# Two tiles of x loaded through the ScalarE queue, and one tile's transposes placed ahead of the first gate matmuls

## The chip, the cores and the metric

The kernel runs on one core of a Trainium2 chip. The metric is device time in microseconds (us) of one execution; the kernel before took 179.11 us as the median of 6 runs (178.76 to 179.28). Names of engines in the profile: PE is TensorE (matmuls, and PEld its weight loads), DVE is VectorE, ACT is ScalarE, POOL is GpSimd, SP is SyncE. DMA transfers are issued either by SP's queue (SPq in the profile) or by ACT's (ACTq).

## The reference

The input is normalised, and two branches work on the normalised rows: a state-space recurrence and a gated feed-forward. The sum of both and the input is the output.

```python
xn = _layernorm(x, axis=-1)                       # x: 1 x 2048 x 512, bf16
# A: 512 complex states; Lam, B, C, dt are parameters
Lam_bar = jnp.exp(dt * Lam)
B_bar = ((Lam_bar - 1.0) / Lam)[:, None] * Bmat
Bu = jnp.einsum("bld,pd->blp", xn + 0j, B_bar)
for t in range(L):                                # L = 2048
    h = Lam_bar[None, :] * h + Bu[:, t, :]
y = 2.0 * jnp.einsum("blp,dp->bld", hseq, Cmat).real + xn * Dskip
# B: w_gate, w_up: 512 x 1376, w_down: 1376 x 512
ffn = (_gelu(xn @ w_gate) * (xn @ w_up)) @ w_down
out = x + y + ffn
```

## The kernel before, in words

The 2048 rows are 16 tiles of 128 rows, taken in four blocks of four tiles. For each block the kernel normalises (LN), transposes the rows through DMA (TR, so that the 512 columns lie on the partitions), multiplies with the gate and up weights (GU), multiplies with B (BU), runs the recurrence as scans on DVE (CHAIN) and multiplies hidden values and states with w_down and C into one accumulation (DN). The blocks are interleaved so that PE always has something to do.

Block 0 can't wait for DMA transposes, so its head goes another way, and the change is in this head only. Each of its tiles j is centred on DVE (`sub`, line 932; for tile 1 line 940, whose mean comes from ACT, line 937), transposed by PE against an identity (`cent_T(j)`, line 673: four 128x128 transposes) and copied from PSUM by ACT (line 680; for tile 0 in two halves, in two banks). Then `GT_mm(j, r, bank, us, ks)` (line 698) multiplies the transposed tile with column range r of the gate (us has 0) or up (us has 1) weights over the quarters ks of the 512 inputs. `GT_evac` (lines 707 and 710) applies gelu on ACT and the product on DVE.

Before the first tile is there PE runs 7 matmuls of 512 columns on zeros (`fwarm`, line 913), and between the first real steps it runs `fill(n)`, n matmuls of 128 columns on zeros into a spare bank (line 920). Their results are not used.

In what follows x0 to x3 are the loads of tiles 0 to 3 (`ld_x0`, line 498, 128 KB each), gate half 0 and gate half 1 the two loads of the first 384 gate columns (`ld_wg0`, line 502, 192 KB each), WU0 the load of the first 384 up columns (line 494). The three small parameter rows (line 518) go through the ACT queue and are transposed by a DMA (`tr_par`, line 522), which SP issues after the weights and before the four transposes of block 0 (TR(0), line 722).

The kernel has its own planner (`Sched`). PE's and SP's instructions run in the order in which the program makes them; those of DVE, ACT and POOL are put in order by a list scheduler that uses a guessed duration for each operation (`dur`) and the dependencies, in six rounds, of which the shortest plan is kept. `order_behind(op, prev)` puts op behind prev on the same engine with no semaphore wait. Waits are made for all other dependencies. `after=[...]` adds a dependency by hand. The gelu on one column at line 480 has no use for its value: it makes ACT load its gelu table early. Its guessed duration is 1480 ns.

The order of PE's head is written by hand:

```python
fill(2)
cent_T(0, tb, "AA")
fill(3)
... # gate, tile 0, quarters 0 and 1, r = 0 and 1
cent_T(1, [wb])
... # gate, tile 0, quarters 2 and 3
fill(6)
...
for r in range(2):
    GT_mm(1, r, ub[1, r], [0])
```

On DVE the head is a chain in fixed order (`ch`): statistics of tile 0, its centring, tile 1's centring, statistics of tile 1, root, statistics and centring of tile 2, reciprocal, two normalisations, tile 3.

Of the kernel before, what the change touches and what calls it, by code (L numbers as in the profile page):

```python
# [10 lines left out]
ACTF = mybir.ActivationFunctionType  # L11
# [356 lines left out]
D_TINY = 160.0  # L368
def d_act(n, ptr=0): return 190.0 + 0.833 * n + 90.0 * ptr
# [3 lines left out]
def build(nc, ins, out):  # L373
    with ExitStack() as es:
        E = es.enter_context
        S = Sched(nc, es)
# [6 lines left out]
        def ring(parent, name, n):  # L383
            return [A.sub(parent, "%s%d" % (name, i), i) for i in range(n)]
# [13 lines left out]
        X = ring(X_all, "X", NT)  # L398
# [18 lines left out]
        HALF = A.alloc("HALF", [4], F32)  # L417
# [11 lines left out]
        PROWq = [Buf("PROW%d" % q, "prow", q, q + 1) for q in range(3)]  # L429
# [39 lines left out]
        x2 = ins["A_x"][0]  # L469

        V = lambda fn, dur, r, w, tag="", after=(): S.op("vector", fn, dur, r, w, tag, after)
        ACT = lambda fn, dur, r, w, tag="", after=(): S.op("scalar", fn, dur, r, w, tag, after)
# [3 lines left out]
        V(lambda e: e.memset(WRM.ap, 0.0), 150, [], [WRM], "wrm")  # L476
        GATE = {"before_gelu": [], "nh": 0}
        SCR = A.alloc("SCR", [1], F32)
        V(lambda e: e.memset(HALF.ap, 0.5), D_TINY, [], [HALF], "half")  # L479
        GATE["table"] = ACT(lambda e: e.activation(SCR.ap, HALF.ap[:, 0:1], ACTF.Gelu_apprx_tanh), 1480, [HALF], [SCR], "gelu0")  # L480
        POOL(lambda e: e.iota(IOT.ap, [[1, 128]], base=0, channel_multiplier=-1), 300, [], [IOT], "iota")
        GATE["ident"] = V(lambda e: e.tensor_scalar(IDN.ap, IOT.ap, 0.0, None, ALU.is_equal), d_dve_ts4x(128), [IOT], [IDN], "ident")
        POOL(lambda e: e.memset(PROW16.ap, 0.0), 100, [], [PROW, *PROWq], "prow0")
# [8 lines left out]
        def ld_w(W, Wc, src, ci, queue="sync", after=()):  # L492
            f0, f1 = FCH[ci]
            return S.dma(lambda e: e.dma_start(W.ap[:, :, f0:f1], src[:, f0:f1].rearrange("(k p) f -> p k f", p=128)),
                         512 * (f1 - f0) * 2, writes=[Wc[ci]], tag="ld_w", queue=queue, after=after)

        def ld_x0(j):
            S.dma(lambda e, j=j: e.dma_start(X[j].ap, x2[128 * j:128 * (j + 1), :]), 128 * 1024, writes=[X[j]], tag="ld_x0")
        WG0h = [Buf("WG0h%d" % n, "sbx", n / 2, (n + 1) / 2) for n in range(2)]

        def ld_wg0(n, queue, after=()):
            return S.dma(lambda e: e.dma_start(WG.ap[:, 2 * n:2 * n + 2, 0:384],
                                        ins["B_w_gate"][256 * n:256 * (n + 1), 0:384].rearrange("(k p) f -> p k f", p=128)),
                  192 * 1024, writes=[WG0h[n]], tag="ld_w", queue=queue, after=after)
        ld_x0(0)
        ld_x0(1)
        ld_wg0(0, "sync")
        ld_wg0(1, "scalar", [GATE["iotj"]])
        ld_x0(2)
        ld_w(WU, WUc, ins["B_w_up"], 0)  # L510
        ld_x0(3)
        for ci in (1, 2):
# [3 lines left out]
        def load_par():  # L516
            for q, nm in enumerate(("A_log_dt", "A_Lambda_re", "A_Lambda_im")):
                S.dma(lambda e, q=q, nm=nm: e.dma_start(PROW.ap[4 * q:4 * q + 4, :], ins[nm].rearrange("(s p) -> s p", p=128)),
                      1024, writes=[PROWq[q]], tag="ld_" + nm, queue="scalar", after=[GATE["iotj"]])

        def tr_par():
            S.dma(lambda e: e.dma_start_transpose(PAR.ap.rearrange("p q t -> p (q t)").unsqueeze(1), PROW16.ap), 4096,
# [34 lines left out]
        def next_bank():  # L557
            b_ = rstate["n"] % 8
            rstate["n"] += 1
            return b_  # L560
# [102 lines left out]
        def cent_T(j, banks, engs="A"):  # L663
            per = KD // len(engs)
            for n, eng in enumerate(engs):
                bank = banks[n]
                pt = PS[bank].bitcast(BF16)

                def f(e, n=n, pt=pt):
                    ins_ = None  # L670
                    for q in range(per):
                        k = per * n + q
                        ins_ = e.transpose(pt[:, 128 * q:128 * (q + 1)], XN[j].ap[:, 128 * k:128 * (k + 1)], IDN.ap)  # L673
                    return ins_
                PE(f, 56.0 * per, [XN[j], IDN], [BANK[bank]], "T0")
                dst = XC_all.ap[:, per * n:per * (n + 1), 128 * j:128 * (j + 1)]
                src = pt[:, 0:128 * per].rearrange("p (q t) -> p q t", q=per)
                w = [XCs[j][n]] if len(engs) == 2 else XCs[j]
                if eng == "A":
                    GATE["evTA"] = ACT(lambda e, src=src, dst=dst: e.activation(dst, src, ACTF.Copy), d_act(128 * per), [BANK[bank]], w, "evT")  # L680
                else:
                    V(lambda e, src=src, dst=dst: e.tensor_copy(dst, src), 110 + 0.6 * 128 * per, [BANK[bank]], w, "evT")
# [3 lines left out]
        def GT_mm(j, r, bank, us, ks=range(KD)):  # L686
            f0, f1 = FR[r]
            w = f1 - f0
            ci = max(0, r - 1)
            Wc = [(WGc, WUc)[u][ci] for u in us]  # L690
            if ci == 0 and us == [0] and len(ks) == 2:
                Wc = [WG0h[ks[0] // 2]]
            dst = PS[bank][:, w * us[0]:w * (us[-1] + 1)].rearrange("p (w f) -> p w f", w=len(us))

            def f(e):
                ins_ = None
                for k in ks:
                    ins_ = e.matmul(dst, XCd(j, k), WGU[:, us[0]:us[-1] + 1, k, f0:f1], start=(k == 0), stop=(k == KD - 1))  # L698
                return ins_
            PE(f, d_pe([w * len(us)] * len(ks)), Wc + XCs[j][ks[0] // 2:ks[-1] // 2 + 1], [BANK[bank]], "GT")  # L700
# [207 lines left out]
        wb = next_bank()  # L908
# [7 lines left out]
        def fill(n):  # L916
            def f(e):
                ins_ = None
                for _ in range(n):
                    ins_ = e.matmul(PS[fb][:, 0:128], WRM.ap, WRM.ap, start=True, stop=True)  # L920
                return ins_
            PE(f, 56.0 * n, [WRM], [BANK[fb]], "fill")
# [8 lines left out]
        def sub(j):  # L931
            return V(lambda e: e.tensor_scalar(XN[j].ap, X[j].ap, MVt[0][j].ap[:, 0:1], None, ALU.subtract),
                     d_dve_ts4x(512), [X[j], MVt[0][j]], [XN[j]], "sub")
        load_par()
        load_W()
        tr_par()
# [9 lines left out]

        fill(2)
        cent_T(0, tb, "AA")
        fill(3)
        ub = {(j, r): next_bank() for j in range(2) for r in range(2)}  # L950
        for r in range(2):
            GT_mm(0, r, ub[0, r], [0], (0, 1))
        cent_T(1, [wb])
        for r in range(2):
            GT_mm(0, r, ub[0, r], [0], (2, 3))
        fill(6)
        for j in range(2):
            ch(norms(0, [j], mn0, rq0, 0))
        ch(*stats(0, 3)); ch(sub(3))
# [64 lines left out]
def bass_parallel_sum__ssm_conv_s5__geglu_ffn__prompt_kernel(  # L1024
    nc: bass.Bass,
    A_x: bass.AP,
    A_Lambda_re: bass.AP,
    A_Lambda_im: bass.AP,
    A_B_re: bass.AP,
    A_B_im: bass.AP,  # L1030
    A_C_re: bass.AP,
    A_C_im: bass.AP,
    A_log_dt: bass.AP,
    A_Dskip: bass.AP,
    B_x: bass.AP,
    B_w_gate: bass.AP,
    B_w_up: bass.AP,
    B_w_down: bass.AP,
    out: bass.AP,
):  # L1040
    ins = {
        "A_x": A_x, "A_Lambda_re": A_Lambda_re, "A_Lambda_im": A_Lambda_im,
        "A_B_re": A_B_re, "A_B_im": A_B_im, "A_C_re": A_C_re, "A_C_im": A_C_im,
        "A_log_dt": A_log_dt, "A_Dskip": A_Dskip,
        "B_w_gate": B_w_gate, "B_w_up": B_w_up, "B_w_down": B_w_down,
    }
    build(nc, ins, out)
# [28 lines left out]
```

## Time and profile before

| what | value |
|---|---|
| median of 6 runs | 179.11 us |
| the profiled execution: time | 178.76 us |
| the profiled execution: span in the trace | 177.0 us |
| PE busy | 173.2 us, 98% of the span |
| DVE busy | 160.7 us, 91% |
| ACT busy | 89.3 us, 50% |
| POOL busy | 10.0 us, 6% |
| DMA moved | 14.36 MB, mean 81 GB/s |

The span goes from the first instruction to the last one of the trace; the execution's own time is 1.76 us more. Times inside the trace count from the span's start. The busy time of PE says that it has work queued nearly always, not what the work is: the warm matmuls and fills of the head count in it too. The page's 40 slices show PE at 9 tenths in all slices but the first (7) and the last (3), and DVE at 9 in most slices after the second. The DMA engines are at 9 tenths in slices 2 to 5, which is 4.4 to 22 us, and mostly at 4 or below after slice 14.

### The profile page before, as it was taken

To read this page: it belongs to the slowest core of one execution; us is meant where nothing else is said; L and a number is where in the kernel's file an instruction comes from. 1 tells how busy PE (TensorE), PEld (TensorE's weight loads), DVE (VectorE), ACT (ScalarE), POOL (GpSimd) and SP (SyncE) were. 2 spreads that over 40 slices of the span, in tenths; PEclk is the share of its full clock that TensorE was granted. 3 is DMA by queue.
4 is the path that set the end of the run, shared out by engine and by line. 5 is a ranking of instruction groups with operands and counts; after the bars stand their busy time and mean duration, and the time that the engine had idled before them with its cause. 6 is when DMAs were issued, how large, how long until landed. Compare 5 with 4: busy or idle time off the path is not lost.

```text
span 177.0 us, 2522 instructions
## 1 busy us (share of the span) xinstructions
PE 173.2 (98%) x893; PEld 84.6 (48%) x893; DVE 160.7 (91%) x283; ACT 89.3 (50%) x169; POOL 10.0 (6%) x25
## 2 busy tenths in 40 slices
PE   7999999999999999999999999999999999999993
PEld 3854464444644444444644444444554444444453
DVE  4989999996999999789999999899999999999911
ACT  4475578989866897003676593000757680000000
POOL 3212030220000000300000000000000000000000
PEclk9999999999999999999999999999999999999999
DMA  5999989286799400011034000100001000000321
GB/s 150 322 323 91 256 203 159 33 162 133 155 196 337 50 0 0 0 61 59 4 66 82 2 0 0 33 30 30 30 0 33 0 0 0 0 0 25 103 86 30
DMA packets 33396, 14.36 MB, mean 81 GB/s; under 512 B 23688, under 2 KB 33384, under 8 KB 33384
## 3 DMA queue, kind: packets, MB, share of 16 engines
q1 hardware_dynamic: 33088, 14.00, 34.7%
q10 hardware_dynamic: 296, 0.20, 0.4%
q8 instruction: 7, 0.11, 0.3%
q14 instruction: 5, 0.04, 0.1%
HBM read 6.46 MB, written 2.10 MB: 48 GB/s over the span
## 4 chain that ended last, share of the span: by engine, by line
PE 98%; DVE 0%; issue 0%
PE PS L863 37%; PE PS L823 32%; PE PS L734 16%; PE PS L698 7%; PE PS L797 3%; PE PS L913 2%; PE PS L673 1%; PE PS L920 0%; DVE arena L881 0%; DVE arena L476 0%; DVE arena L479 0%
## 5 line engine op out<-in xcount | busy, mean ns | idle before, releaser
L863 PE MATMUL PS<-arena 128*128 128x512 bf16 (+3 forms) x323 | 66.2, 366 | 0.0
L823 PE MATMUL PS<-arena 128*128 128x512 bf16 x264 | 58.1, 379 | 0.0
L863 PEld LDWEIGHTS PS<-arena 128*128 128x128 bf16 (+1 forms) x323 | 30.9, 98 | 35.2
L823 PEld LDWEIGHTS PS<-arena 128*128 128x128 bf16 x264 | 25.8, 98 | 30.4
L767 DVE TENSOR_TENSOR_SCAN arena<-arena 128x512 bf16<-128x512 f32 x32 | 38.7, 1250 | 0.0
L838 ACT ACTIVATE arena<-PS 128x512 bf16<-128x512 f32 x33 | 19.8, 600 | 37.4 <-PE PS L823 32.9
L734 PE MATMUL PS<-arena 128*128 128x512 bf16 x128 | 28.1, 379 | 0.0
L841 ACT ACTIVATE arena<-PS 128x512 bf16<-128x512 f32 x33 | 19.9, 602 | 5.0 <-PE PS L823 5.0
L734 PEld LDWEIGHTS PS<-arena 128*128 128x128 bf16 x128 | 12.5, 98 | 14.9
L855 ACT ACTIVATE PS<-arena 128x512 f32<-128x512 bf16 (+2 forms) x17 | 9.3, 580 | 17.5 <-DVE arena L881 17.1
L738 ACT ACTIVATE arena<-PS 128x512 bf16<-128x512 f32 x32 | 17.4, 599 | 1.2 <-PE PS L734 1.0
L881 DVE TENSOR_TENSOR arena<-PS,arena 128x512 bf16<-128x512 f32 (+2 forms) x17 | 10.9, 654 | 7.6 <-PE PS L863 7.4
L843 DVE TENSOR_TENSOR arena<-arena 128x512 bf16<-128x512 bf16 x33 | 13.0, 411 | 1.9 <-ACT arena L841 1.9
L698 PE MATMUL PS<-arena 128*128 128x192 bf16 (+2 forms) x80 | 13.0, 315 | 0.1
L624 DVE BATCH_NORM_STATS2 arena<-arena 128x6 f32<-128x512 bf16 x16 | 10.2, 681 | 1.2 <-DMA arena<-in_A_x_dram 1.2
L698 PEld LDWEIGHTS PS<-arena 128*128 128x128 bf16 x80 | 7.2, 98 | 4.9 <-issue 0.3
L756 DVE TENSOR_TENSOR arena<-arena 128x4096 bf16<-128x4096 bf16 (+1 forms) x5 | 9.2, 1861 | 0.1
L754 DVE TENSOR_TENSOR arena<-arena 128x4096 bf16<-128x4096 bf16 (+1 forms) x5 | 9.2, 1854 | 0.0
L780 DVE TENSOR_TENSOR arena<-arena 128x4096 bf16<-128x4096 bf16 x4 | 9.1, 2283 | 0.0
L779 DVE TENSOR_TENSOR arena<-arena 128x4096 bf16<-128x4096 bf16 x4 | 9.1, 2282 | 0.0
L707 ACT ACTIVATE arena<-PS,arena 128x192 bf16<-128x192 f32 (+1 forms) x16 | 6.7, 449 | 3.0 <-PE PS L698 3.0
L710 DVE SCALAR_TENSOR_TENSOR arena<-PS,arena 128x192 bf16<-128x192 f32 (+1 forms) x16 | 6.9, 447 | 1.1 <-ACT arena L707 0.6
(84 smaller groups left out, 110.6 us busy)
## 6 DMA issues: line engine op xcount, KB each, us to landing
out_dram<-arena SPq DMA_DIRECT2D x15, 128.0 KB, 1.7
arena<-in_A_x_dram SPq DMA_DIRECT2D x3, 512.0 KB, 5.0
arena<-in_B_w_down_dram SPq DMA_DIRECT2D x1, 1280.0 KB, 7.9
arena<-in_A_x_dram SPq DMA_DIRECT2D x4, 128.0 KB, 2.7
arena<-in_B_w_gate_dram SPq DMA_DIRECT2D x2, 256.0 KB, 4.8
arena<-in_B_w_up_dram SPq DMA_DIRECT2D x2, 256.0 KB, 5.1
arena<-in_B_w_gate_dram SPq DMA_DIRECT2D x1, 480.0 KB, 5.6
arena<-in_B_w_up_dram SPq DMA_DIRECT2D x1, 480.0 KB, 5.9
```

The lines of the kernel that those rows point to most:

```text
L624: return (V(lambda e: e.bn_stats(ST[tt].ap, X[tt].ap), d_dve_1x(512), [X[tt]], [ST[tt]], "bnst"), V(lambda e: e.bn_aggr(MVt[b][j].ap, ST[t ...
L698: ins_ = e.matmul(dst, XCd(j, k), WGU[:, us[0]:us[-1] + 1, k, f0:f1], start=(k == 0), stop=(k == KD - 1))
L734: ins_ = e.matmul(PS[bank][:, :], BBT[c][dk].ap[:, 128 * s:128 * (s + 1)], XNT[b].ap[:, dk, :], start=(dk == 0), stop=(dk == KD - 1))
L738: ACT(lambda e, bank=bank, k3=k3, s=s, c=c: e.activation(SSc[k3][s][c].ap, PS[bank][:, :], ACTF.Copy), d_act(512), [BANK[bank]], [SSc[k3][ ...
L767: V(lambda e, g=g, rb=rb, init=init: e.tensor_tensor_scan(g.ap, rb, g.ap, init, ALU.mult, ALU.add), d_dve_scan(512), [g, PA[RRr]] + ([CARc ...
L823: ins_ = e.matmul(PS[bank][0:m, c0:c1], W.ap[:, dk, 128 * ft:128 * ft + m], XNT[b].ap[:, dk, c0:c1], start=(dk == 0), stop=(dk == KD - 1))
L838: GATE["last_gelu"] = ACT(lambda e, bg=bg, kk=kk, m=m: e.activation(GG[kk].ap[0:m, :], PS[bg][0:m, :], ACTF.Gelu_apprx_tanh), d_act(512), ...
L841: ACT(lambda e, bu=bu, kk=kk, m=m: e.activation(UPB[kk].ap[0:m, :], PS[bu][0:m, :], ACTF.Copy), d_act(512), [BANK[bu]], [UPB[kk]], "evU")
L843: V(lambda e, kk=kk, m=m, ft=ft, k2=k2: e.tensor_tensor(HTt[k2][ft].ap[0:m, :], GG[kk].ap[0:m, :], UPB[kk].ap[0:m, :], ALU.mult), d_dve_tt ...
L855: ACT(lambda e: e.activation(PS[bank][:, c0:c1], X[tt].ap[:, c0:c1], ACTF.Copy), d_act(c1 - c0), [X[tt]], [BANK[bank]], "seed")
L863: ins_ = e.matmul(PS[bank][:, c0:c1], l_[:, 128 * j:128 * (j + 1)], r_[:, c0:c1], start=False, stop=last and n == len(ops) - 1, skip_group ...
L881: V(lambda e: e.tensor_tensor(OUTB[ko].ap[:, c0:c1], PS[bank][:, c0:c1], XD[tt].ap[:, c0:c1], ALU.add), d_dve_1x(c1 - c0), [BANK[bank], XD ...
```

## The change

Three things are changed, all in the head.

1. x1 and x2 are issued from the ACT queue, ordered behind the table gelu, instead of from SP's. Gate half 1 goes the other way, from the ACT queue (where it waited for `iotj`, an iota on POOL) to SP's. SP's order is then x0, gate half 0, gate half 1, WU0, x3 and so on.
2. The three parameter rows wait for `half` (a memset on DVE) instead of for `iotj`, beside the memset of their target, which stays. The table gelu's guessed duration goes from 1480 to 100 ns; the instruction is the same.
3. On PE tile 1's transposes go ahead of tile 0's gate matmuls, in the place of `fill(3)`, and `fill(6)` becomes `fill(4)`.

```diff
-        V(lambda e: e.memset(HALF.ap, 0.5), D_TINY, [], [HALF], "half")
-        GATE["table"] = ACT(lambda e: e.activation(SCR.ap, HALF.ap[:, 0:1], ACTF.Gelu_apprx_tanh), 1480, [HALF], [SCR], "gelu0")
+        half = V(lambda e: e.memset(HALF.ap, 0.5), D_TINY, [], [HALF], "half")
+        GATE["table"] = ACT(lambda e: e.activation(SCR.ap, HALF.ap[:, 0:1], ACTF.Gelu_apprx_tanh), 100, [HALF], [SCR], "gelu0")
...
-        def ld_x0(j):
-            S.dma(lambda e, j=j: e.dma_start(X[j].ap, x2[128 * j:128 * (j + 1), :]), 128 * 1024, writes=[X[j]], tag="ld_x0")
+        def ld_x0(j, queue="sync", after=()):
+            return S.dma(lambda e, j=j: e.dma_start(X[j].ap, x2[128 * j:128 * (j + 1), :]), 128 * 1024, writes=[X[j]], tag="ld_x0", queue=queue, after=after)
...
         ld_x0(0)
-        ld_x0(1)
+        S.order_behind(ld_x0(1, "scalar"), GATE["table"])
         ld_wg0(0, "sync")
-        ld_wg0(1, "scalar", [GATE["iotj"]])
-        ld_x0(2)
+        ld_wg0(1, "sync")
+        S.order_behind(ld_x0(2, "scalar"), GATE["table"])
         ld_w(WU, WUc, ins["B_w_up"], 0)
         ld_x0(3)
...
-                      1024, writes=[PROWq[q]], tag="ld_" + nm, queue="scalar", after=[GATE["iotj"]])
+                      1024, writes=[PROWq[q]], tag="ld_" + nm, queue="scalar", after=[half])
...
         fill(2)
         cent_T(0, tb, "AA")
-        fill(3)
+        cent_T(1, [wb])
         ub = {(j, r): next_bank() for j in range(2) for r in range(2)}
         for r in range(2):
             GT_mm(0, r, ub[0, r], [0], (0, 1))
-        cent_T(1, [wb])
         for r in range(2):
             GT_mm(0, r, ub[0, r], [0], (2, 3))
-        fill(6)
+        fill(4)
```

## The prediction

> **What bounds the kernel now.** I read the chain of work that ended last first, then PE's waits, then the head instruction by instruction on PE, DVE and ACT, then the DMA. By the chain PE holds 98% of the span. Its pieces in the head (start, duration, what):
>
> ```profile
> 4.37 0.46 PE PS L673 x4
> 4.83 0.24 PE PS L920 x3
> 5.07 0.11 issue
> 5.18 0.49 PE PS L698 x4
> 5.67 0.22 PE PS L673 x4
> 5.89 0.33 PE PS L698 x4
> 6.22 0.34 PE PS L920 x6
> 6.56 0.02 issue
> 6.58 1.17 PE PS L698 x12
> ```
>
> L673 are transposes, L698 real matmuls, L920 fills. From 6.58 to 174.3 the chain has no step off PE. The list of PE's waits has one entry in the whole span, the start:
>
> ```profile
> PE PS L913 <- DVE arena L479: 1.0, 1, 1.0
> ```
>
> So time can be won only ahead of 6.58, where fills and holes are not work, and can be lost anywhere. What releases PE there is on ACT and DVE (start, duration, engine, line):
>
> ```profile
> 3.39 0.63 ACT L937 ACTIVATE arena<-arena 128x512 bf16<-128x512 bf16 x1 [1.16 <-DMA arena<-in_A_x_dram]
> 3.93 0.18 ACT L937 ACTIVATION_READ_ACCUMULATOR arena<-arena 128x1 f32 x1
> 4.22 0.35 DVE L940 TENSOR_SCALAR arena<-arena 128x512 bf16<-128x512 bf16 x1
> 4.65 0.38 ACT L680 ACTIVATE arena<-PS 128x256 bf16<-128x256 bf16 x1 [0.54 <-PE PS L673]
> 4.93 0.38 ACT L680 ACTIVATE arena<-PS 128x256 bf16<-128x256 bf16 x1
> 5.93 0.60 ACT L680 ACTIVATE arena<-PS 128x512 bf16<-128x512 bf16 x1 [0.62 <-PE PS L673]
> ```
>
> Tile 1: x1's landing, its mean on ACT (to 4.11), centring on DVE (to 4.57). Centred tile 1 then lies idle until 5.50, when its transposes start. Their copy ends at 6.53, and tile 1's matmuls start at 6.58: fill(6) (to 6.56) only covers that wait. The first gate matmul (5.18) waits for tile 0's first copy, done at 5.03.
>
> **The change, part by part.** The sum is made in the profiled execution (178.76 us, span 177.0, 0.35 under the median of the runs); I carry its difference to the median, 179.11.
>
> *PE's order.* Tile 0's transposes stay where they are, to 4.83. Tile 1's follow at once, 0.22 by their own row, to 5.05. They sit in the 0.35 that fill(3) and the hole take, so gate matmuls still start at 5.18: 0.13 behind the transposes. First quarters 0.49 (to 5.67), second 0.33 (to 6.00), with the 0.22 between them gone. fill(4) is 4 x 0.34/6 = 0.23, to 6.23. Tile 1's copy: transposes end at 5.05, ACT is free for the next copy 0.28 after 4.93 (the spacing of its first two), so 5.21 to 5.81, below 6.23. Tile 1's matmuls start at 6.23 instead of 6.58: 0.22 + 2 x 0.057 + 0.02 = **0.35 won**.
>
> *x1's landing decides whether that holds.* The trace's semaphore updates put landings at 2.84 (x0, issued 0.74), 3.37 (x1, issued 1.19), 4.72 and 4.96 (gate halves 0 and 1), 5.29 (x2). Centred tile 1 is there 4.57 - 3.37 = 1.20 after x1, and PE needs 0.06 more (4.16 to 4.22 for tile 0). Transposes that start at landing + 1.26 end at landing + 1.48; the gate matmuls move only when that is past 5.18, so a landing up to 3.70 costs nothing. Past it PE stands still us for us, and at 3.70 + 0.35 = 4.05 the gain is gone. Behind the mean's wait for x1 on ACT stand tile 0's copies: they start at 4.65, and the mean's 0.72 ends by then for a landing up to 3.93.
>
> *The ACT queue.* It waits for `half` (0.88 to 0.94), so x1 is issued at some 1.0. The table load doesn't hold it:
>
> ```profile
> 0.74 1.28 ACT L480 ACT_TABLE_LOAD   x1 [0.74 <-PEq L1061]
> 1.61 0.50 ACTq L502 DMA_DIRECT2D arena<-in_B_w_gate_dram  x1
> 2.03 0.20 ACT L480 ACTIVATE arena<-arena 128x1 f32<-128x1 f32 x1
> ```
>
> The queue issued at 1.61, in the load, and the gelu still ran right behind the load: it had been handed on earlier. With x1's old time from issue to landing, 2.18, it lands at 3.2. But the one large transfer that this queue carried is a bad sign: gate half 1 had its first packet at 3.59, 1.98 after issue, against 1.04 for x0 on SP's queue. With 1.98 and x0's 1.06 from first packet to landing, x1 lands at 4.04; with gate half 1's whole 3.35, at 4.35. What was late there? Stretches of the head, with the DMA engines' share and GB/s last:
>
> ```profile
> 1.80:2.80 1.00, 1.00 (x4) 0.43 (x3) 0.00 (x0) 0.42 (x2) 0.56 (x4) 1.00 0.78 234
> 2.80:3.40 0.60, 0.60 (x3) 0.17 (x2) 0.54 (x1) 0.01 (x1) 0.00 (x0) 1.00 0.73 124
> 3.40:5.00 1.60, 1.60 (x11) 0.96 (x9) 1.47 (x5) 1.06 (x4) 0.00 (x0) 1.00 1.06 344
> ```
>
> From 2.8 to 3.4 SP's own gate packets were slow too (some took 0.3 to 0.5 us against 0.036 later), so part of that delay is the weights' first read, not the queue. In the new order that slow first read comes beside x1, no longer behind it. I take 3.2 to 3.7, with 3.5 as the value, nearest to x1's own row, and keep 4.35.
>
> [...]
>
> *x0* is still first, but x1's packets may mix with its own (1.78 to 2.3). Bounds: 0 if they queue behind, 0.26 if the half of x0 that is left at 2.04 is slowed twofold. The engines' share there was 0.78, so there is room: I take 0. Tile 0's centring ends at 4.16 and its transposes start at 4.22, so little covers a delay.
>
> *The other transfers.* SP issues one fewer ahead of WU0, so WU0 is issued some 0.45 earlier; it landed at 6.85 and is needed by the ninth of the twelve matmuls after 6.58, at 6.58 + 8 x 0.0975 = 7.36, in future at 7.01. Gate half 1 becomes SP's third: even as last of five it lands at 5.29, needed at 5.67. x2 is needed by the statistics at 5.51 and has at most the same bytes ahead of it. The parameter rows go out in one go behind x2 (0.63 + 0.26 + 0.26, to about 3.2), ahead of the mean's wait. That frees SP:
>
> ```profile
> SPq L340 <- DMA arena<-in_A_Lambda_im_dram: 0.8, 1, 0.8
> ```
>
> The parameter transpose waited 0.8 for the last row; behind it stand TR(0)'s four, whose last landed at 17.28 and is needed at 18.69. Off the path: worth 0.
>
> *The rest moves along.* Everything that I checked follows PE or has room: block 1's transposes land at 30.98, needed at 25.19 + 13.81/2 = 32.10; the last CHAIN ends at 161.40, its states are needed at 157.83 + 22 x 0.216 = 162.58 (DN(3) starts 32.91/2 after 141.41). Both follow PE's work in turn, so a start 0.35 earlier takes little of the 1.1 us.
>
> *Guessed durations* cost nothing themselves, but DVE, ACT and POOL are ordered by the planner, and a different plan may come out for all three. Bounds: 0 if the order stands; else one long DVE operation put ahead of CHAIN(3), 2.28 (line 754's row), less the 1.18 of room: +1.1. I take 0, because PE's order doesn't change after the head.
>
> **The rivals.**
> - *x1 lands between 3.7 and 4.05* on the ACT queue: the gain shrinks to 0 to 0.3. At 4.04, 0.34 of it is lost: 179.1. For it: the 1.98. Against: slow SP packets in the same stretch. Here belongs the case that the change doesn't do what it says, an x1 no earlier than on SP's queue. Chance 0.27.
> - *x1 lands past 4.05*: slower. Place: tile 1's transposes, now ahead of gate matmuls that could run without x1. At 4.35 they end at 5.83, tile 1's matmuls start at 5.83 + 0.49 + 0.33 + 0.23 = 6.88: +0.30, 179.4. DVE's chain stands still for 4.35 - 3.37 = 0.98 too, and the product of unit (0,0), whose bank tile 3's transposes take, moves from 9.4 to 10.4 against 10.1 before. The two don't add. Chance 0.14.
> - *Another plan lets PE wait once* in a later block: up to 179.11 + 1.1 - 0.35 = 179.9; deciding is whether the order of DVE differs around a CHAIN. For it: the six rounds pick the shortest plan, and small shifts can flip it. Against: PE's one wait in 177 us leaves all margins above. Chance 0.17.
>
> **How the numbers follow.** The forecast, x1 in time and no new wait, has 0.42: 179.11 - 0.35 = 178.76, own range 178.4 to 178.95 (0.46 if the other 0.11 of hole went too, with 0.25 for the spread of runs; 0.15 lost to x0 or to ACT's order). A difference of 0.2%, 0.36 us, is about what a measurement of this kernel tells from none, and the forecast lies just at it: I put most of its chance on faster, as the hole ahead of the matmuls may shrink too: 0.36, and 0.06 on the same. The first rival gives 0.05 faster, 0.18 same, 0.04 slower (with the 0.26 of x0 on top); the second 0.12 slower, 0.02 same; the third 0.14 slower, 0.02 same, 0.01 faster. Together: faster 0.42, same 0.28, slower 0.30. Range: 178.3 to 179.7; it leaves out the worst plans and the luckiest runs.
>
> **What would show it.** Right: transposes of tile 1 directly behind tile 0's, ending by 5.2; x1's first packet at 2.1 to 2.4; tile 1's matmuls at 6.2; SP's wait for the last parameter row gone; PE's waits still one. Wrong: the mean on ACT starting after 3.7, a hole in PE ahead of tile 1's transposes, any wait of PE for DVE or ACT past 10 us.

## The result, and the profile after

The changed kernel took 178.33 us as the median of 18 runs (177.88 to 178.85), the kernel before 179.06 (39 runs, 178.72 to 179.45). The ratio is 0.9963, with a 95% interval of 0.9955 to 0.9971: 0.73 us between the medians, about twice the 0.35 that was forecast. A second measurement gave 0.9955 (0.9939 to 0.9971).

The profiled execution of the changed kernel doesn't show this at first sight: it took 178.71 us, with a span of 177.2, longer than the 177.0 before. Here is its head on PE (start, duration, line, tile and count, and in brackets the idle time before and what ended it):

```profile
4.38 0.66 PE L673 MATMUL PS<-arena 128*128 128x128 bf16 x8
5.23 1.12 PE L698 MATMUL PS<-arena 128*128 128x192 bf16 x8 [0.19 <-ACT arena L680]
6.19 0.39 PE L920 MATMUL PS<-arena 128*128 128x128 bf16 x4
6.41 0.82 PE L698 MATMUL PS<-arena 128*128 128x192 bf16 x8
7.58 0.50 PE L698 MATMUL PS<-arena 128*128 128x192 bf16 x4 [0.35 <-DMA arena<-in_B_w_up_dram]
```

Tile 1's transposes are right behind tile 0's (the eight of the first line), and tile 1's gate matmuls start at 6.41 instead of 6.58. But the next step, the up matmuls, waits until 7.58. The second line's eight gate matmuls have a hole in their middle, and the weight loads (PEld) name its cause, a late gate half 1:

```profile
5.84 0.28 PEld L698 LDWEIGHTS PS<-arena 128*128 128x128 bf16 x4 [0.35 <-DMA arena<-in_B_w_gate_dram]
```

The chain that ended last no longer begins on PE. It goes through a transfer (start, duration, what):

```profile
2.17 5.37 DMA arena<-in_B_w_up_dram
7.54 0.05 issue
7.58 0.50 PE PS L698 x4
8.09 0.22 PE PS L673 x4
8.31 2.29 PE PS L698 x20
```

WU0 was issued at 2.17 instead of 2.63 and landed at 7.54 instead of 6.85. From here to the end PE is as gapless as before. Its two issues, before and after:

```profile
2.63 0.43 SPq L494 DMA_DIRECT2D arena<-in_B_w_up_dram  x1
2.17 0.47 SPq L494 DMA_DIRECT2D arena<-in_B_w_up_dram  x1
```

On ACT the queue issued x1 and x2 early and the parameter rows behind them:

```profile
0.91 0.87 ACTq L498 DMA_DIRECT2D arena<-in_A_x_dram  x2
1.82 0.58 ACTq L518 DMA_DIRECT2D arena<-in_A_log_dt_dram  x1
2.43 0.27 ACTq L518 DMA_DIRECT2D arena<-in_A_Lambda_re_dram  x1
2.72 0.37 ACTq L518 DMA_DIRECT2D arena<-in_A_Lambda_im_dram  x1
3.31 0.63 ACT L937 ACTIVATE arena<-arena 128x512 bf16<-128x512 bf16 x1 [1.07 <-DMA arena<-in_A_x_dram]
```

x1 was issued at 0.91 and landed at 3.29 (issued at 1.19, landed at 3.37 before); the mean starts right behind it.

Two things make the rest readable. First, **everything between the first up matmul and the landing of the last store is of fixed length**. It took 168.85 to 168.90 in eleven of the fourteen profiles of this document (168.85 before, 168.87 after). The three others are the second and seventh experiment, where PE waited later on, and the eighth, where work was moved ahead of that matmul. So the head alone decides, plus what comes behind the last store.

Second, **what comes behind the last store is not a constant**. From its landing to the end of the execution it is 2.65 before (178.76 - 176.11) and 2.25 after (178.71 - 176.46): **0.4 us of the 0.73 are won after all work is done**. A part of it lies outside the span: the execution's time less its span is 1.79 us before (178.76 - 176.97) and 1.53 after (178.71 - 177.18). SP's waits at line 374, where the program ends, show the place. Before:

```profile
SPq L374 <- PEq L374: 0.2, 1, 0.2
```

and after:

```profile
SPq L374 <- SPq L374: 0.5, 1, 0.5
```

In the kernel before SP is held 0.47 between its last branch (176.21) and its closing drain (176.68), and 0.22 behind the drain; in the changed one 0.14 and 0.46. SP's program in the trace has 81 instructions before and 80 after: x1 and x2 have left it, gate half 1 has come. (The wait's line alone doesn't tell the two apart: the ninth, eleventh and twelfth experiment show that of the kernel before with the short end.)

### The profile page after: what moved, and what is told of

The parts are those of the page before. It is cut to its first block, busy times and chain, and to the rows that moved or that the text cites. A ratio compares the mean times of both kernels' runs of the same rounds, so it can differ in the third digit from the quotient of the medians.

```text
span 177.2 us, 2507 instructions
## 1 busy us (share of the span) xinstructions
PE 172.9 (98%) x888; PEld 83.9 (47%) x888; DVE 160.9 (91%) x283; ACT 89.3 (50%) x169; POOL 10.1 (6%) x25
## 4 chain that ended last, share of the span: by engine, by line
PE 94%; DMA 3%; SPq 1%; DVE 0%; issue 0%
PE PS L863 37%; PE PS L823 32%; PE PS L734 16%; PE PS L698 6%; DMA arena<-in_B_w_up_dram 3%; PE PS L797 3%; SPq L502 0%; PE PS L673 0%; SPq L498 0%; DVE arena L881 0%
```

## The experiments

Theory A was the prediction's: the gain is made by PE's order. Theory B: by the transfers. Theory C: by the planner's other plan. The experiments ran in four groups, each on one chip beside runs of the kernel before on that chip: 1 to 4 (median of the kernel before 179.24), 5 to 8 (179.06), 9 to 11 (179.12) and 12 (178.94). So across groups the ratios are to be compared, not the times.

**1. The queues, the rows' wait and the guessed duration, with PE's order of before.**

Against the changed kernel:

```diff
-        cent_T(1, [wb])
+        fill(3)
...
+        cent_T(1, [wb])
...
-        fill(4)
+        fill(6)
```

> The change's queues, parameter waits and guessed duration, with PE's order of before (fill(3), tile 1's transposes between the gate matmuls, fill(6)). Theory A, the gain is made on PE: PE's hand-written order sets the head as before, tile 1's matmuls start at 6.6, time 179.06, ratio 0.999 to 1.001. Theory B, the gain is made by the transfers (ordinary runs of before wait for a transfer that its profiled run had in time): 178.4 to 178.8, ratio 0.9965 to 0.9985. Theory C, the planner's other order of DVE, ACT and POOL makes it: the whole gain is here, 178.3 to 178.5.

Measured: 178.59, ratio 0.9969 (0.9955 to 0.9982). By the number theory B. But the span in the profile is only 0.2 shorter than before, tile 1's matmuls start at 6.51 against 6.58, and time less span is 1.53: of the 0.5 won (0.54 between the means) 0.4 are behind the last store, and 0.1 to 0.15 in the head.

**2. PE's order alone.**

```diff
         cent_T(0, tb, "AA")
-        fill(3)
+        cent_T(1, [wb])
...
-        cent_T(1, [wb])
...
-        fill(6)
+        fill(4)
```

> PE's new order alone (tile 1's transposes behind tile 0's, no fill(3), fill(4)); queues, waits and guessed duration of before. Theory A: x1 lands at 3.37 as before, in time for transposes at 4.83, so tile 1's matmuls start at 6.23 and the up weights land at 6.85, ahead of their need at 7.01: 0.35 won, 178.7, ratio 0.9975 to 0.9985. Theory B: PE reaches the up weights sooner than they land in many runs, 0 to 0.2 won, 178.9 to 179.1. Theory C: nothing but what its own plan brings, 179.0 to 179.1.

Measured: 179.69, ratio 1.0025 (1.0011 to 1.0040): slower, which none of the theories expected. Tile 1's matmuls do start at 6.38, but WU0 lands at 7.29, and more is lost later. The profiled execution took 180.03, 0.34 more than the median, so it shows more than the typical loss. PE's waits:

```profile
PE PS L797 <- ACT arena L738: 0.5, 1, 0.5
PE PS L734 <- DMA arena<-arena: 0.3, 1, 0.3
```

SP's wait for the parameter rows has grown from 0.8 to:

```profile
SPq L340 <- DMA arena<-in_A_Lambda_im_dram: 1.4, 1, 1.4
```

and the chain that ended last has these pieces:

```profile
2.63 4.66 DMA arena<-in_B_w_up_dram
...
17.25 4.06 DMA arena<-in_A_x_dram
21.33 1.29 DVE arena L624 x2
...
28.85 3.38 DMA arena<-arena
32.23 0.25 issue
32.48 6.20 PE PS L734 x28
```

With the new order the planner put the last parameter row behind tile 1's copy on ACT: it was issued at 5.28 instead of 4.87, and SP's wait for it ended at 9.80. The parameter transpose was issued at 9.89 instead of 9.09, and what SP had behind it came later: block 1's x was issued at 17.25 instead of 16.07, its statistics waited for it, its transposes (the DMA at 28.85) followed, and PE waited 0.3 for them in BU(1). But the late row is not shown to be the cause. It accounts for 0.8 of the 1.2 by which x is late. Just ahead of 17.25 the chain goes through DVE's line 611 and not through the row, and PE's longer wait, 0.5 for ACT at 45.9, isn't explained by it.

**3. The changed kernel again.** No edit.

> The changed kernel a second time, for a second profile. If the late up weights (7.54) and gate half 1 (5.80) of its first profile are the luck of one run, this one shows them 0.3 to 0.7 earlier and a span near 176.6; if they belong to the new queues, they land at 7.4 or later again and PE waits for them again, 0.3 to 0.6. Time 178.33 either way, ratio 0.9955 to 0.997.

Measured: 178.32, ratio 0.9955 (0.9939 to 0.9971), span 176.8. Gate half 1 lands at 5.20 and WU0 at 7.11. PE's waits:

```profile
PE PS L698 <- DMA arena<-in_B_w_up_dram: 0.3, 1, 0.3
PE PS L698 <- ACT arena L680: 0.2, 1, 0.2
```

So the first profile had an unlucky landing, but the wait for the up weights can come again with the changed kernel's head. Against the first experiment, mean against mean, PE's order on top of the new queues is worth 178.63 - 178.36 = 0.27; each mean is uncertain by about 0.09, so this is good to some 0.12.

**4. The kernel before again.** No edit.

> The kernel before against itself: ratio 1.000 within 0.001. For a second profile: theory B expects a transfer later than in the first (up weights past 7.36 or gate half 1 past 5.7) and a wait of PE for it, span 177.3; theory A expects the same head as in the first profile, no wait of PE for a transfer, span 177.0.

Measured: 179.05, ratio 0.9999 (0.9985 to 1.0013), span 177.4. Neither expectation: no wait for a transfer, and yet tile 1's matmuls start at 7.01 instead of 6.58. PE itself was slower:

```profile
4.69 0.53 PE L920 MATMUL PS<-arena 128*128 128x128 bf16 x3
5.25 0.80 PE L698 MATMUL PS<-arena 128*128 128x192 bf16 x4
```

These four matmuls took 0.49 in the first profile. After the first two their starts are 0.160 us apart here, 0.082 there. The short spacing begins at about 6.0 in this execution and at 4.85 in the first; more on this at the end.

**5. The kernel before with one transfer fewer in SP's program.** Theory D: the stretch behind the last store goes with the length of SP's program.

```diff
-... 96 * 1024, writes=[WDc[1]], tag="ld_wd")
+... 96 * 1024, writes=[WDc[1]], tag="ld_wd", queue="scalar", after=[GATE["last_gelu"]])
```

> The kernel before, with one transfer fewer in SP's program: the last 96 rows of w_down, needed at 64 us, are issued by ACT behind block 0's gelus. Head as before. Theory D, part of the gain lies behind the last store and goes with the length of SP's program: from the last landing to the end of the execution 2.25 instead of 2.65, time 178.7, ratio 0.997 to 0.9985. Rival, that stretch goes with the ACT queue carrying x: 2.65 stays, 179.06, ratio 0.999 to 1.001.

Measured: from the last landing to the end 2.25 (178.60 - 176.35), and time less span 1.53 as a median over its runs. SP's wait at the end is that of the changed kernel:

```profile
SPq L374 <- SPq L374: 0.5, 1, 0.5
```

Theory D, although x stays on SP's queue. The time was 178.87 and the ratio 0.9987 (0.9962 to 1.0012): not clear of no change, since the runs' spans don't show the 0.13 that is saved inside them (median 177.35, 177.3 for the kernel before): their heads were some 0.2 later, and why isn't shown.

**6. The changed kernel with one transfer more in SP's program.**

```diff
-            ld_x(3)
+            for h in range(2):
+                ... # tiles 12 + 2h and 13 + 2h, 256 KB
```

> The changed kernel with one transfer more in SP's program: block 3's x is loaded as two halves, at some 51 us where SP has time. Theory D: from the last landing to the end 2.65 again, time 178.7, ratio 0.997 to 0.999. Rival, that stretch goes with the ACT queue carrying x: 2.25 stays, 178.33, ratio 0.9955 to 0.997.

Measured: 2.66 (179.16 - 176.50), time less span 1.79, and the wait of the kernel before:

```profile
SPq L374 <- PEq L374: 0.2, 1, 0.2
```

Time 179.00, ratio 0.9984 (0.9960 to 1.0007): one more transfer, far from the path at 51 us, takes back half of the change and more. Experiments 5 and 6 with the two kernels make a square. Means: before 179.13 with 81 instructions on SP and 178.94 with 80; changed 178.95 with 81 and 178.38 with 80. SP's length is worth (0.19 + 0.57)/2 = 0.38, the head (0.18 + 0.56)/2 = 0.37. Each mean is uncertain by about 0.09, and the fourth pools the first measurement and the third experiment, which did not run beside the three others, so the split is good to about 0.1 at best; the two halves of each sum differ by more. The 0.4 itself was read directly in the profiles. Taken from the 0.73 (0.66 between the means) it leaves 0.26 to 0.33 for the head.

**7. PE's order with the early parameter rows, x1, x2 and gate half 1 on their old queues.** Theory E: the second experiment lost by the late row. Against the kernel before, with the second experiment's edit beside this one:

```diff
-... Gelu_apprx_tanh), 1480, [HALF], [SCR], "gelu0")
+... Gelu_apprx_tanh), 100, [HALF], [SCR], "gelu0")
...
-... queue="scalar", after=[GATE["iotj"]])
+... queue="scalar", after=[half])
```

> PE's new order as in the second experiment (179.69), with the parameter rows' new wait and the guessed duration too; x1, x2 and gate half 1 stay on their old queues. Theory E, the second experiment lost because its last parameter row was issued at 5.29 and held up SP's transposes of block 0: the rows go out before 3.2, the parameter transpose is issued by 9.2 instead of 9.89, PE waits for nothing past 10 us, and the shorter head shows: 178.8, ratio 0.997 to 0.9995. Rival, PE's order can't gain with x1 on SP's queue: 179.3 or more, ratio over 1.001.

Measured: 179.13, ratio 1.0003 (0.9973 to 1.0033). Between the two expectations. The rows go out by 2.81, the parameter transpose at 8.67, and some 0.4 of the second experiment's time is back (the ratio 1.0025 has become 1.0003). But nothing is won. The profiled execution (179.60, 0.47 over the median) waits:

```profile
PE PS L734 <- DMA arena<-arena: 0.4, 1, 0.4
PE PS L698 <- DMA arena<-in_B_w_gate_dram: 0.3, 1, 0.3
PE PS L698 <- DMA arena<-in_B_w_up_dram: 0.2, 1, 0.2
```

Gate half 0 lands at 5.51 and WU0 at 7.43. On the old queues gate half 0 stands behind x1; in the five profiles with this order it landed at 4.72 to 5.51, in the nine with the new one at 3.99 to 4.87. BU(1) waits for block 1's transposes besides, 0.4 here against 0.3 in the second experiment, although block 1's x went out at 15.27 here and at 17.25 there. So that wait doesn't hang on the late row; the room of 1.1 that the prediction named there was used up by this plan. What is gone is the wait of 0.5 for ACT. Row and guessed duration were changed together, so theory E is not shown.

**8. The changed kernel with tile 2's transposes ahead of the first up matmuls.**

```diff
             GT_mm(1, r, ub[1, r], [0])
+        cent_T(2, tb)
         for j in range(2):
...
-                if j == 0 and r == 0:
-                    cent_T(2, tb)
```

> The changed kernel with tile 2's transposes (0.22) ahead of the first up matmuls instead of behind the first four of them. Theory F, the head of the changed kernel now ends with a wait for the up weights (0.29 to 0.57 in both profiles): the transposes fill it, up matmuls start when the weights land, and where these are late 0.2 is won: 178.1 to 178.25, ratio to before 0.9945 to 0.9955. Rival, the wait is rare outside the profiles: 178.33, no change.

Measured: 178.38, ratio 0.9962 (0.9938 to 0.9986): no gain over the changed kernel's 0.9963 is seen, though the interval also holds what theory F expected. In its profile WU0 landed at 6.86, ahead of need, and x0 only at 3.13, so there was no wait to fill.

**9. The changed kernel with one transfer fewer in SP's program** (79 instructions; the edit of the fifth experiment).

> The changed kernel with one transfer fewer in SP's program (the last 96 rows of w_down issued by ACT): two fewer than in the kernel before. Theory D1, each instruction less shortens the end: from the last landing to the end under 2.0, time 177.9 to 178.1, ratio 0.993 to 0.995. Theory D2, the length only decides on which instruction of the end a fixed delay falls: 2.25 stays (or 2.65 comes back), 178.33 (or 178.7).

Measured: 178.17 (6 runs), ratio 0.9957 (0.9940 to 0.9974). From the last landing to the end 2.26 (178.23 - 175.97): theory D2. The span is 0.3 shorter behind the drain, and the time outside the span 0.27 longer (1.80): the same delay, fallen behind the trace's last instruction.

**10. The changed kernel without fill(4).**

> The changed kernel without fill(4): tile 1's gate matmuls follow tile 0's at once. Theory F, the head now ends with the up weights' landing (7.1 to 7.5): PE waits longer for them instead, 178.3, ratio 0.9955 to 0.9965. Rival, in executions where PE's clock becomes full late (after 5.5) the fills are on the path, 0.2 to 0.4 each time: 178.15 to 178.25 on average, ratio 0.995.

Measured: 178.38 (5 runs), ratio 0.9963 (0.9950 to 0.9976). That is what theory F expected, but the rival's 0.995 is the interval's end and not excluded. In its profile, 0.35 over the median, WU0 lands at 7.53, and PE waits 0.4 for it.

**11 and 12. No fill(4), no fill(2), and the edit of the ninth experiment**, run twice.

> Both of these, and fill(2) left out too, as a candidate. Theory F: what the ninth experiment gives and nothing more, 178.3 (D2) or 178.0 (D1). Rival: 0.1 to 0.2 less than the ninth experiment.

> The eleventh experiment's kernel a second time, since its interval rests on five runs. If leaving out fill(2) and fill(4) wins by itself, 177.9 to 178.1 again (ratio 0.9935 to 0.9945), below the 178.33 of the changed kernel; if it was the luck of five runs, 178.2 to 178.4.

Measured: 177.93 (5 runs), ratio 0.9937 (0.9925 to 0.9949), then 178.12 (10 runs), 0.9951 (0.9938 to 0.9965). Some 0.25 below the changed kernel by the ratios, and the fastest of all that ran. But the second time lies between the two expectations, 0.02 above the range that was expected of a real gain, and its interval holds the changed kernel's 0.9963: the gain over the changed kernel is likely, not shown. Which of the three edits does it wasn't separated.

## Why the prediction was right, and what it missed

The way and the place in the head were right; the size was luck in part. The measured 178.33 lies below the forecast's own range (178.4 to 178.95) and only just inside the whole one (from 178.3), because 0.4 of the gain come from a stretch that the sum held fixed.

- *PE's order*, 0.35 forecast. The mechanism is right: tile 1's transposes in the place of fill(3), and the same start of the gate matmuls (5.18 forecast; 5.23 and 5.17). In the four profiles with the changed kernel's head (after and experiments 3, 6 and 9) tile 1's matmuls start at 6.41, 6.05, 6.99 and 6.42, on average 6.47; in the three with the head of before (before and experiments 4 and 5) at 6.58, 7.01 and 6.83, on average 6.81. At the first up matmul 0.11 of these 0.34 are left (7.37 against 7.48 on average), since late weights take some back; these are few profiles. Over many runs PE's order is worth 0.27 on top of the new queues (experiment 3 against 1), and the whole head 0.26 to 0.37. That is the forecast's size, partly by accident. An estimate from the spacings at the end: where the clock is late, each fill left out saves 0.107 instead of 0.056. The 0.22 for tile 1's transposes is their row at the short spacing; in experiment 6, before the switch, they took 0.43. And the order needs the new queues: alone (experiments 2 and 7) it wins nothing.
- *x1's landing*, 3.2 to 3.7 forecast: 3.29 and 3.26, and 3.16 to 3.49 in all nine profiles with the new queues. Its first packet came at 2.18, inside the 2.1 to 2.4 that were named as the sign. It lands hardly earlier than on SP's queue (3.20 to 3.38 in five profiles) although it is issued 0.28 earlier; no step needed it earlier. Its first packet is 1.27 behind its issue, so gate half 1's 1.98 in the kernel before was not the queue's own delay, and both rivals on x1 fall.
- *x0*, put at 0 within bounds of 0 to 0.26: it landed at 2.77 to 3.20 with the new queues and at 2.81 to 2.96 with the old, 0.09 later on average. Tile 0's transposes start 1.38 behind it in thirteen of the fourteen profiles, so at worst (experiment 9) they began at 4.58 instead of 4.22. The term is small, not 0.
- *WU0*, "issued some 0.45 earlier", needed at 7.01: this step failed. It was issued 0.47 earlier and landed no earlier: 6.80 to 7.43 in five profiles with the old queues, 6.57 to 7.54 in nine with the new ones (on average 7.13 and 7.04). The same 768 KB were issued ahead of it in both kernels (x0 to x2 and the two gate halves), and from 3.4 to 7 us the DMA engines' busy share was 1.00 to 1.10 before and 0.97 to 1.03 after; that these bytes set its landing is an estimate, which no run shows by itself. The need was mis-sized besides: eight matmuls took 0.67 (6.58 to 7.25), not 0.78, so by the forecast's own order WU0 is needed at 6.90. PE waits for it in four of the nine, and the sign "PE's waits still one" did not come true.
- *Gate half 1*, "even as last of five it lands at 5.29": 5.03 to 6.05, and later than 5.29 in six of the nine. PE waited some 0.3 for it in the profile after and in that of experiment 6. The bound took the rate of one profile as certain.
- *The parameter rows*, "worth 0": right in the changed kernel's sum, and SP's wait for the last of them is gone as forecast. The prediction named the cover (TR(0), room 1.4) and not that a new plan can issue the row later still, as in experiment 2; how much of that experiment's loss is the row's stays open.
- *The sum's frame*: "I carry its difference to the median". The stretch around the span was taken as fixed; it moved by 0.4. This is the missing half of the gain, and it has nothing to do with what the kernel computes.
- *Another plan*: DVE's and ACT's order differ in many places, and the length behind the first up matmul stayed the same. The rival fell for the changed kernel; it did happen in experiments 2 and 7.

## What to carry to other kernels

Make the sum for the whole execution: compare the stretch from the last landing to the end before crediting an edit in the head, and change the transfer count of the issuing engine alone as a control. Go by a transfer's landing, not by its issue: here x1 was issued 0.28 earlier on another queue and WU0 0.47 earlier with the same bytes ahead of it, and they landed at 3.29 instead of 3.37, and at 7.04 instead of 7.13 on average. And a profile shows one execution: put its time beside the median before a wait in it is called the cause, and take a second profile of the same kernel on both sides.

## What the runs showed of the hardware

**The end of the program.** With 81 instructions on SP the last landing to the end took 2.65 to 2.68 us in five profiles (before, experiments 2, 4, 6, 7), with 80 or 79 it took 2.25 to 2.29 in nine, whichever kernel it was. The square of experiments 5 and 6 shows that SP's length is the lever. In the eleven profiles with 81 or 80 one closing step is long, 0.46 instead of 0.14 to 0.22, and it is always the one ahead of SP's 80th instruction in the trace: with 81 that is the closing drain, with 80 the last event behind the drain. With 79 no step inside the trace is long, but 0.27 more lies outside the span. With 81 such a 0.27 outside comes on top. One packet of the kind "instruction" (8 KB, the last on DMA queue 14) follows in each trace, 1.16 to 1.20 us behind the last landing with 81 instructions, 1.33 to 1.35 with 80 and 1.51 to 1.54 with 79. So the delay keeps its place in SP's program. Its cause was not tested, and no other lengths were tried.

**The clock's start.** The granted clock stands at 1.00 in all rows of these heads, yet transposes of 128 columns start 0.107 us apart at first and 0.056 later, matmuls of 192 columns 0.160 and 0.082. The rows don't show the slow stretch because the trace's own record of the clock begins only at the switch, in eleven of the fourteen profiles (at 4.85 us in the profile before, at 4.03 after; the three others have no record). The switch came at 3.74 us in one execution (experiment 3) and at 6.82 in another (experiment 6), with PE busy from 1.0 on in both. The eight transposes of the first line took 0.66 in the profile after; in the sixth experiment:

```profile
4.25 1.03 PE L676 MATMUL PS<-arena 128*128 128x128 bf16 x8
5.21 1.70 PE L701 MATMUL PS<-arena 128*128 128x192 bf16 x8
```

(lines are 3 further down there). The two switches are 3.08 apart; what decides the moment isn't shown. In the three profiles with the head of before, which waited for no weights, the first up matmul starts at 7.25, 7.50 and 7.68 with the switch at 4.85, about 5.7 and about 6.0 (the latter two estimated from the spacing). By these three it can account for an estimated 0.43 (7.68 - 7.25) of the 0.7 to 1.0 us between runs of one kernel; that was not tested by itself.

**Early reads.** In the stretch from 1.75 to 7 us the transfers run mostly at 200 to 380 GB/s per quarter of a microsecond; from 7.25 us on it is 318 to 355. With the old queues all five profiles have a hole between 3.0 and 3.5 us (28 to 92 GB/s in its lowest quarter); with the new queues none of the nine has it (205 and more there). The prediction shows the row of before, with 124 GB/s; after it is

```profile
2.80:3.40 0.60, 0.60 (x3) 0.20 (x2) 0.37 (x1) 0.09 (x1) 0.00 (x0) 1.00 1.10 284
```

With the new queues gate half 0 and x2 also land earlier (3.99 to 4.87 instead of 4.72 to 5.51, and 4.46 to 5.06 instead of 5.23 to 5.80). But in the two first profiles the lead is lost again by 7 us: from 1.8 on 1.46 MB had been moved before, 1.45 after. What makes the hole isn't shown. Single packets of 0.2 to 1.0 us stand among those of 0.036 to 0.046, at other places in each execution, and in the nine profiles with the new queues the landings of the first weights vary by 0.9 to 1.0 us, more than the whole change is worth.
